# Token tile 3 normalised from the transposed copy of x, query weights loaded later, one exponential behind a copy, one warm-up product fewer

## The chip, the cores and the metric

The kernel runs on one core of one Trainium2 chip. The metric is device time in microseconds (us) of one execution; the median of three runs stands for a kernel. The engines are TensorE (PE in the profile, its weight loads PEld), VectorE (DVE), ScalarE (ACT), GpSimd (POOL) and SyncE (SP), which here only issues transfers.

## The reference

x has 2048 tokens of 640 numbers. A linear attention with 32 heads of 20 and a gated MLP read the same layer norm of x:

```python
x = A_x
xn = _layernorm(x, axis=-1)
s = _A_ref(xn, A_wqkv, A_w_phi, A_wo)
g = _silu(_B_ref(xn, B_w1, B_b1, B_w2, B_b2))
return x + s * g
```

with, in `_A_ref`, after `q, k, v` have been made from `xn @ wqkv` and `pq`, `pk` from `q` and `k` by the head's matrix `w_phi`:

```python
phi_k = jnp.concatenate([_softmax(pk, axis=-1), _softmax(-pk, axis=-1)], axis=-1)   # phi_q alike
kv = jnp.einsum("bhsf,bhsd->bhfd", phi_k, v)
z  = jnp.einsum("bhsf->bhf", phi_k)
num = jnp.einsum("bhqf,bhfd->bhqd", phi_q, kv)
den = jnp.einsum("bhqf,bhf->bhq", phi_q, z)[..., None] + 1e-6
o = num / den
```

`_B_ref` is `gelu(xn @ w1 + b1) @ w2 + b2` with 1536 hidden numbers. All inputs are float32.

## The kernel before

Tokens are worked in 16 tiles of 128, tile t being half of pair q = t // 2 (`at(q)` is the pair's place). Products are made in split form: each operand is a high part (rounded, `AF.Copy` on ScalarE into float32r) and a low part (the rest, a subtraction on VectorE or GpSimd), and `PASSES` adds high x high, high x low and low x high. In `project` a block of x is the weight side: for each of five blocks, four passes read its high part and then two its low part. The order of instructions is written out by hand on every engine in this part of the program (`tc.manual_schedule`), so each engine works in the order of the code.

The start of the program, up to about 240 us of the profile, is attention:

- Nine products of ones by ones (L521) run first on TensorE. The key weights are folded with `w_phi` on TensorE (`fold`, L174) from `wkT`, loaded by `load_fold(1, ...)`; the right side is a block matrix `foldb` that VectorE makes (L542) of the loaded `bd`.
- Tiles 0 to 3 are loaded as rows of tokens (`x_in`), normalised there (`norm_a`/`norm_b`/`norm_act`; L246 is the VectorE form), transposed on TensorE (`transpose_x`, L363) and split from PSUM (`plain`, L285 and L287). Tile 3 goes through `norm(3)` and is transposed within the value projection of tile 1.
- Tiles 4 and later come in pairs: `load_xr` brings x already transposed, `pair_stats` makes mean and reciprocal root (the power of -1/2 on GpSimd, L233) from the row copy, writes them to `st_dram` (L337) and reads them back broadcast to all partitions (`bc`, L339); `pair_sub` (GpSimd, L346) and `pair_mul` (VectorE, L351) normalise, `pair_plain` splits.
- A key tile: `project` (L377), `feat1` (VectorE: maximum L389, difference L392, minimum L395; GpSimd: the negated half L396), `feat2` (exponential on ScalarE, L405), `key_fin` (sums L413 and reciprocal L445 on VectorE, scaling L418 on GpSimd). A value tile: `project`, then a copy (L434). `kv_pair` multiplies the two (L457).
- The query weights, `wqT = load_fold(0, ...)`, are loaded near the head of SP's queue, after tiles 1 to 5 and the value weights; `fold_pair` first reads them after tile 4.
- Tiles 10 to 15 make their values by a shorter scheme in pairs (`token_pair`, L685), into whose seven parts other work is hung by `hooks`. Hook 1 is `rest`: the negated half of the later key, the exponential of the first, and more. The value copy of part 2 (L694) comes behind it on ScalarE.

After that stand the MLP (L924 first layer, L953 second layer) and the output projection (L1111), which the change doesn't touch.

```python
vs[1] = value(1, lambda: transpose_x(3))
phis[1] = key_fin(es.pop(1))
vf = [v_forms(0), v_forms(1)]
for t in range(2, 6):
    pk = project(t, wk_s)
```

Of the kernel before, what the change touches and what calls it, by code (L numbers as in the profile page):

```python
# [15 lines left out]
P = 128  # L16
# [13 lines left out]
NH = 2  # L30
# [16 lines left out]
def hedgehog_gated_mlp_kernel(ctx: ExitStack, tc: tile.TileContext, x, xt_in, wqk, bd, wv, wo, w1, b1, w2, b2, out_t):  # L47
# [39 lines left out]
    def bankA():  # L87
        return pools["A"].tile([P, 2, 512], F32, tag="A", name="pA")
# [72 lines left out]
    def load_fold(which, engs):  # L161
        tl = folds[:, which]
        for c, eng in enumerate(engs):
            if c == 1 and which:
                x_in(0, nc.scalar)
            eng.dma_start(tl[:, c], wqk[which, c, :, :6 * P].rearrange("p (i t) -> p i t", i=6))
        return tl
# [185 lines left out]
    def pair_plain(q):  # L353
        for o in range(2):
            plain(q, o, xrs[q][:, :, o * P:(o + 1) * P])

    def transpose_x(t):
        q, o = divmod(t, 2)
        xn = xns.pop(t)
        ps = bankA()  # L360
        flat = ps[:].rearrange("p a b -> p (a b)")
        for k in range(KC):
            nc.tensor.transpose(flat[:, k * P:(k + 1) * P], xn[:, k * P:(k + 1) * P], ident[:])  # L363
        plain(q, o, flat[:, :D].rearrange("p (k t) -> p k t", t=P))
# [148 lines left out]
    def x_in(t, eng=None):  # L513
        xts[t] = load_x(t, eng)
# [1 line left out]
    phase1 = ExitStack()  # L516
    phase1.enter_context(tc.manual_schedule(engines={mybir.EngineType.PE, mybir.EngineType.SP}))
    one = nc.const_aps.tensor(1.0, [P, P], F32)
    for pw in (bankA(), bankA(), bankA()):
        for i in range(3):  # L520
            nc.tensor.matmul(pw[:, 0, :P], one, one, start=True, stop=True)  # L521
    startup = ExitStack()
    startup.enter_context(tc.manual_schedule())
# [4 lines left out]
    wv_raw = [load_raw(wv[c * P:(c + 1) * P, :]) for c in range(KC)]  # L528
    for t in (3, 4, 5):
        x_in(t)  # L530
    wqT = load_fold(0, (nc.sync,) * KC)
    x_in(6)
    x_in(7)
    nc.sync.dma_start(b1t[:], b1)
# [25 lines left out]
    es[0] = feat1(pk)  # L560
    split_v(3)
    pk = project(1, wk_s, lambda: transpose_x(2))
    load_xr(2)
    load_xr(3)
    x_in(8)
    x_in(9)
    load_xr(4)
    split_v(4)
    feat2(es[0])
    norm(3)  # L570
    es[1] = feat1(pk)
    pair_stats(4)
    vs[0] = value(0)
    pair_stats(5)
    phis[0] = key_fin(es.pop(0))
    feat2(es[1])
    vs[1] = value(1, lambda: transpose_x(3))
    phis[1] = key_fin(es.pop(1))
    vf = [v_forms(0), v_forms(1)]
    for t in range(2, 6):  # L580
        pk = project(t, wk_s)
        if t % 2:
            kv_pair(t - 3)
        es[t] = feat1(pk)
        if t == 4:
            next(vf[0])
        if t == 2:
            pair_sub(2)
            pair_stats(6)
            pair_stats(7)  # L590
            pair_mul(2)
        if t == 3:
            pair_plain(2)
        if t > 3:
            pair_stats(t + 4)
        if t in (3, 4, 5):
            spill(t - 3)
        if t == 5:
            x_in(10)
        if t == 4:  # L600
            pair_sub(3)
            pair_mul(3)
        vs[t] = value(t, (lambda: transpose_x(t + 2)) if t < 2 else None)
        if t >= 4:
            fold_pair(t - 4)
        if t == 5:
            next(vf[0])
        feat2(es[t])
        if t == 4:
            pair_plain(3)  # L610
        phis[t] = key_fin(es.pop(t))
# [182 lines left out]
    for p in range(5, 8):  # L794
# [21 lines left out]
        def rest(t=t, p=p):  # L816
            if p == 5:
                nc.scalar.dma_start(e_dram[_tok(queries_done.pop(0))], ef)
                next(vb)
                next(vb, None)  # L820
            later.pop(0)()
            feat2(es[t])
            if p == 6:
                t_sums(7)
            if p == 7:
                next(qf)

# [10 lines left out]
            if p == 6:  # L838
                t_split(7)

        value_pair(p, {1: rest, 2: lambda: p == 7 and next(qf), 3: lambda: p == 5 and pair_sub(7), 4: first_key, 6: second_key})
    w1f = w1_forms(w1r)

    def early_rest(q, ea):
# [522 lines left out]
```

## Time and profile before

| | |
|---|---|
| median of three runs | 651.21 us (651.04 to 651.24) |
| the profiled execution | 651.21 us |
| its span, first to last instruction | 649.3 us |
| granted TensorE clock, mean | 0.999 |
| busy: PE, DVE, ACT, POOL | 644.2, 483.1, 237.9, 406.8 us |
| DMA | 136.07 MB, mean 210 GB/s |

A row of the timeline reads: start in us, length in us, engine, line, operation, what is written `<-` what is read, shapes, how many were merged, and in brackets how long the engine was idle before and what ended that. A row of the chain reads: start, length, engine, tile, line, count. In a row of waits stand the waiting engine, tile and line, `<-` the one waited for, total us, times, and the longest. A row of a table by stretches has the stretch, its length, busy time and count of PE, PEld, DVE, ACT and POOL, the granted clock, the DMA share and GB/s. SPq and ACTq are the issuing sides of those engines, on which a row is the issue alone.

### The profile page before, as it was taken

Reading aid. Unit: us, or ns where it says so; the run is one execution under the profiler, and the core shown is the slowest. Engines: PE = TensorE matmul, PEld = TensorE weight load, DVE = VectorE, ACT = ScalarE, POOL = GpSimd, SP = SyncE. Lnnn points to the kernel's source line nnn. Section 1 sums busy time; section 2 is a strip of 40 time slices with the busy share of each in tenths; the row PEclk is TensorE's granted clock in tenths of the full one; section 3 lists DMA queues with packets and bytes.
Section 4 is the critical chain, followed back from the end, with each engine's and each line's share of the span. In section 5 each row is a group of like instructions: output and inputs, shape, how many; then the busy total and the mean of one; then the engine's idle time right before and its main releaser. Section 6 shows DMA issues by size and latency. Waiting matters only on the chain.

```text
span 649.3 us, 11414 instructions
## 1 busy us (share of the span) xinstructions
PE 644.2 (99%) x4384; PEld 559.6 (86%) x4384; DVE 483.1 (74%) x736; ACT 237.9 (37%) x345; POOL 406.8 (63%) x373
## 2 busy tenths in 40 slices
PE   9999999999999999999999999999999999999997
PEld 9999999999999998888888888888888886766866
DVE  5886976789777887587988877768889899853232
ACT  3522423325243447144243356642231524032130
POOL 2776477897986756857878875455462966343321
PEclk9999999999999999999999999999999999999999
DMA  8918186494312477365987999694969499999952
GB/s 346 327 18 220 43 299 200 114 300 148 123 42 66 160 263 254 111 213 172 311 234 246 253 411 280 136 344 181 184 228 251 63 279 207 319 244 244 275 192 81
DMA packets 166175, 136.07 MB, mean 210 GB/s; under 512 B 89714, under 2 KB 130162, under 8 KB 165738
## 3 DMA queue, kind: packets, MB, share of 16 engines
q1 hardware_dynamic: 163386, 123.76, 65.7%
q10 hardware_dynamic: 2736, 11.60, 4.7%
q8 instruction: 34, 0.56, 0.4%
q14 instruction: 19, 0.16, 0.1%
HBM read 86.95 MB, written 48.38 MB: 208 GB/s over the span
## 4 chain that ended last, share of the span: by engine, by line
PE 97%; DVE 2%; ACT 0%; issue 0%; POOL 0%; DVEq 0%; POOLq 0%
PE pB L953 24%; PE pA L377 23%; PE pB L924 23%; PE pB L1111 11%; PE pA L685 6%; PE pA L174 2%; PE pB L1058 2%; PE kv L457 2%; PE qV L685 1%; PE qY L685 1%; PE pA L521 1%; DVE y L962 1%; PE pB L1065 1%; PE pA L363 0%; DVE wolh L1035 0%; DVE den L1012 0%
## 5 line engine op out<-in xcount | busy, mean ns | idle before, releaser
L953 PE MATMUL pB<-hs,w2s 128*128 128x512 f32 x720 | 165.8, 389 | 0.0
L953 PEld LDWEIGHTS pB<-hs,w2s 128*128 128x128 f32 x720 | 135.0, 188 | 28.8 <-DVE y L962 0.8
L924 PE MATMUL pB<-xp,w1s 128*128 128x512 f32 x324 | 81.2, 389 | 0.0
L924 PE MATMUL pB<-xd,w1s 128*128 128x512 f32 x324 | 79.3, 389 | 0.0
L1111 PE MATMUL pB<-oT,wo 128*128 128x512 f32 (+1 forms) x315 | 72.3, 381 | 0.0
L418 POOL TENSOR_TENSOR eq<-eq,rc 128x1280 f32<-128x1280 f32 x16 | 37.9, 2370 | 54.6 <-DVE rc L1015 36.7
L924 PEld LDWEIGHTS pB<-xd,w1s 128*128 128x128 f32 x324 | 60.8, 188 | 12.6
L924 PEld LDWEIGHTS pB<-xp,w1s 128*128 128x128 f32 x324 | 60.8, 188 | 12.6
L1111 PEld LDWEIGHTS pB<-oT,wo 128*128 128x128 f32 x315 | 57.2, 188 | 13.8 <-PE pB L1058 2.5
L962 DVE TENSOR_TENSOR y<-pB,y 128x512 f32<-128x512 f32 x100 | 63.1, 675 | 1.4 <-PE pB L953 1.4
L929 ACT ACTIVATE pB<-pB,b1t 128x512 f32<-128x512 f32 x48 | 31.8, 662 | 78.7 <-DVE pB L1192 28.9
L405 ACT ACTIVATE e<-e 128x1280 f32<-128x1280 f32 x32 | 40.8, 1273 | 52.2 <-POOL e L396 52.2
L377 PE MATMUL pA<-wk,xp 128*128 128x320 f32 x384 | 59.6, 310 | 0.0
L396 POOL TENSOR_TENSOR e<-nr,e 128x640 f32<-128x640 f32 x32 | 45.6, 1425 | 20.3 <-DVE nr L395 20.2
L377 PEld LDWEIGHTS pA<-wk,xp 128*128 128x128 f32 x384 | 56.9, 188 | 0.1
L418 POOL TENSOR_TENSOR e<-e,rc 128x1280 f32<-128x1280 f32 x16 | 37.9, 2372 | 19.1 <-DVE rc L445 19.1
L1002 POOL TENSOR_TENSOR ez<-eq,zrep 128x1280 f32<-128x1280 f32 x16 | 47.3, 2957 | 2.7 <-DMA eq<-e_dram 2.7
L485 POOL TENSOR_TENSOR w1s<-raw,w1s 128x640 fp32r<-128x640 f32 (+1 forms) x18 | 26.3, 1460 | 27.0 <-ACT w1s L484 27.0
L377 PE MATMUL pA<-wv,xp 128*128 128x320 f32 x240 | 37.2, 310 | 0.0
L1114 POOL TENSOR_TENSOR xres<-gt,xres 128x256 f32<-128x256 f32 x20 | 14.3, 736 | 35.3 <-DVE gt L1113 35.3
L149 POOL TENSOR_TENSOR w2s<-raw,w2s 128x640 fp32r<-128x640 f32 x23 | 36.0, 1587 | 0.2 <-ACT w2s L147 0.2
L377 PEld LDWEIGHTS pA<-wv,xp 128*128 128x128 f32 x240 | 35.5, 188 | 0.1
(182 smaller groups left out, 1137.2 us busy)
## 6 DMA issues: line engine op xcount, KB each, us to landing
raw<-in_w_dram SPq DMA_DIRECT2D x42, 320.0 KB
e_dram<-e ACTq DMA_DIRECT2D x16, 640.0 KB
eq<-e_dram SPq DMA_DIRECT2D x16, 640.0 KB
phi_t<-eq SPq DMA_DIRECT2D x64, 160.0 KB
phT<-phi_t SPq DMA_DIRECT2D x20, 480.0 KB
xt<-in_x_dram SPq DMA_DIRECT2D x16, 320.0 KB
xres<-in_xt_dram SPq DMA_DIRECT2D x20, 256.0 KB
out_dram<-xres SPq DMA_DIRECT2D x18, 256.0 KB
```

The source lines that it names most:

```text
L149: eng.tensor_tensor(sl[:, 1, :], raw, sl[:, 0, :].bitcast(F32), op=OP.subtract)
L377: nc.tensor.matmul(ps[:, hf, :HALF], stat_x(q, o, k, a), ws[k][:, b, hf * HALF:(hf + 1) * HALF], start=n == 0, stop=n == 3 * KC - 1)
L396: rest = lambda: nc.gpsimd.tensor_tensor(e5[:, :, :, 1, :], nr[:, :, :, None].to_broadcast([P, 2, 16, DH]), e5[:, :, :, 0, :], op=OP.subtract)
L405: nc.scalar.activation(ef, ef, AF.Exp)
L418: nc.gpsimd.tensor_tensor(e3, e3, rc[:, :, None].to_broadcast([P, 64, DH]), op=OP.mult)
L685: nc.tensor.matmul(bank[ch], q_x(blk, a, q), p_weight(base, f, w, k)[:, b], start=ch not in seen and n == 0, stop=n == len(mms) - 1, skip_ ...
L924: nc.tensor.matmul(bank[ch][:], tl[:, a, off + wo_:off + wo_ + P], mov(blk, b), start=new and n == 0, stop=n == len(mms) - 1, skip_group_c ...
L929: nc.scalar.activation(ps, ps, AF.Gelu_apprx_tanh, bias=b1t[:, f:f + 1])
L953: nc.tensor.matmul(ps[:], ws[i][:, b, d * P:(d + 1) * P], hs[o][i][:, a, :], start=i == n == 0, stop=(i, n) == (GF - 1, 2), skip_group_che ...
L962: nc.vector.tensor_tensor(y, ps[:], y, op=OP.add)
L1002: nc.gpsimd.tensor_tensor(zv, ef, zf, op=OP.mult)
L1111: nc.tensor.matmul(ps[:, mv], w, o[:, mv], start=n == 0, stop=n == 15, skip_group_check=True)
```

## The change

1. Tile 3 is no longer normalised as rows and transposed. Its half of the transposed x is loaded (`one_load`), its statistics go through DRAM and come back broadcast (`one_stats`), GpSimd subtracts (`one_sub`), VectorE multiplies and the split is made from SBUF (`one_plain`). The five transposes are gone.
2. The query weights, the rows of tiles 8 and 9 and the transposed x of pairs 3 and 4 are asked for behind the statistics of tile 3 and of pair 2.
3. In the value pairs the first key's exponential moves from hook 1 to hook 2, behind the copy of part 2. For pair 7 a step of the query forms moves with it.
4. Eight products of ones instead of nine.

```diff
+    def one_load(t):
...
+        nc.sync.dma_start(xr[:, :, :P], src)
+        xrs[t, "one"] = xr[:, :, :P]
+
+    def one_stats(t):
+        sm = small.tile([P, 16], F32, tag="st", name="st")
+        ps = small.tile([P, 2], F32, tag="ps1", name="ps1")
+        stats(t, sm, ps[:, 0:1], ps[:, 1:2])
+        nc.sync.dma_start(st_dram[t // 2, t % 2], ps[:])
+        bc = row([P, P, 2], F32, "bc")
+        nc.sync.dma_start(bc[:].rearrange("p t s -> p (t s)"),
+                          st_dram[t // 2, t % 2].rearrange("p s -> (p s)").partition_broadcast(P))
+        pld[t, "one"] = bc
+
+    def one_sub(t):
+        bc, xr = pld[t, "one"], xrs[t, "one"]
+        nc.gpsimd.tensor_tensor(xr, xr, bc[:, None, :, 0].to_broadcast([P, KC, P]), op=OP.subtract)
+
+    def one_plain(t):
+        bc, xr = pld.pop((t, "one")), xrs.pop((t, "one"))
+        nc.vector.tensor_tensor(xr, xr, bc[:, None, :, 1].to_broadcast([P, KC, P]), op=OP.mult)
+        plain(t // 2, t % 2, xr)
...
-    for pw in (bankA(), bankA(), bankA()):
-        for i in range(3):
+    for pw, n in ((bankA(), 3), (bankA(), 3), (bankA(), 2)):
+        for i in range(n):
...
-    wqT = load_fold(0, (nc.sync,) * KC)
...
+    one_load(3)
     load_xr(2)
-    load_xr(3)
-    x_in(8)
-    x_in(9)
-    load_xr(4)
     split_v(4)
     feat2(es[0])
-    norm(3)
+    one_stats(3)
     es[1] = feat1(pk)
     pair_stats(4)
     vs[0] = value(0)
     pair_stats(5)
+    one_sub(3)
+    wqT = load_fold(0, (nc.sync,) * KC)
+    x_in(8)
+    x_in(9)
+    load_xr(3)
+    load_xr(4)
     phis[0] = key_fin(es.pop(0))
     feat2(es[1])
-    vs[1] = value(1, lambda: transpose_x(3))
+    vs[1] = value(1)
     phis[1] = key_fin(es.pop(1))
+    one_plain(3)
...
             later.pop(0)()
-            feat2(es[t])
             if p == 6:
                 t_sums(7)
+            if p == 7:
+                next(qf)
+
+        def copied(t=t, p=p):
+            feat2(es[t])
             if p == 7:
                 next(qf)
...
-        value_pair(p, {1: rest, 2: lambda: p == 7 and next(qf), 3: lambda: p == 5 and pair_sub(7), 4: first_key, 6: second_key})
+        value_pair(p, {1: rest, 2: copied, 3: lambda: p == 5 and pair_sub(7), 4: first_key, 6: second_key})
```

On VectorE, between the sums of keys 0 and 1 (`rc`) and the maximum of key 2 (`mx`), there stands before (`b_298` is the part of the pair's high and low halves kept beside `xp`, `pA` a PSUM bank):

```order
L413 TENSOR_REDUCE rc<-e 128x64
L445 RECIPROCAL rc<-rc 128x64
L287 TENSOR_TENSOR b_298<-pA,b_298 128x2x128
L287 TENSOR_TENSOR xp<-pA,xp 128x3x128
L413 TENSOR_REDUCE rc<-e 128x64
L445 RECIPROCAL rc<-rc 128x64
L389 TENSOR_REDUCE mx<-pA 128x32
```

and after the change, at the same place:

```order
L440 TENSOR_REDUCE rc<-e 128x64
L472 RECIPROCAL rc<-rc 128x64
L440 TENSOR_REDUCE rc<-e 128x64
L472 RECIPROCAL rc<-rc 128x64
L381 TENSOR_TENSOR xr<-xr,bc 128x5x128
L287 TENSOR_TENSOR b_292<-xr,b_292 128x2x128
L287 TENSOR_TENSOR xp<-xr,xp 128x3x128
L416 TENSOR_REDUCE mx<-pA 128x32
```

The two low parts of tile 3 read `xr` in SBUF where they read `pA` in PSUM, a multiplication precedes them, and all three stand behind both keys' sums.

On GpSimd, from the power of -1/2 for tiles 4 and 5 (`pst`) to the scaling of key 1, there stands before:

```order
L233 TENSOR_TENSOR pst<-pst,mhalf 128x1
L427 MEMSET v 128x32
L428 MEMSET v 128x32
L233 TENSOR_TENSOR pst<-pst,mhalf 128x1
L418 TENSOR_TENSOR e<-e,rc 128x1280
```

and now:

```order
L233 TENSOR_TENSOR pst<-pst,mhalf 128x1
L454 MEMSET v 128x32
L455 MEMSET v 128x32
L233 TENSOR_TENSOR pst<-pst,mhalf 128x1
L377 TENSOR_TENSOR xr<-xr,bc 128x5x128
L445 TENSOR_TENSOR e<-e,rc 128x1280
```

The subtraction of tile 3 stands ahead of the scaling of key 0, and so of all that follows.

On SP, from the last loads of x rows at the start, there stands before (`folds` are the query weights, `xr` the transposed x, `st_dram` and `bc` the statistics' way out and back):

```order
L142 DMA xt<-in_x_dram 128x640 x3
L166 DMA folds<-in_wqk_dram 128x768 x5
L142 DMA xt<-in_x_dram 128x640 x2
L534 DMA b1t<-in_b_dram 128x12
L535 DMA b2t<-in_b_dram 128x5
L266 DMA xr<-in_xt_dram 128x5x128
```

and now:

```order
L142 DMA xt<-in_x_dram 128x640 x5
L560 DMA b1t<-in_b_dram 128x12
L561 DMA b2t<-in_b_dram 128x5
L362 DMA xr<-in_xt_dram 128x5x128
L266 DMA xr<-in_xt_dram 128x5x128
L267 DMA xr<-in_xt_dram 128x5x128
L369 DMA st_dram<-ps_370 128x2
L371 DMA bc<-st_dram 128x256
L337 DMA st_dram<-pst 128x2x2
L339 DMA bc<-st_dram 128x512
L166 DMA folds<-in_wqk_dram 128x768 x5
```

The query weights come behind two write-and-read pairs of statistics, the first of them tile 3's.

6 lines of the change are left out of this document (5 added, 1 removed).

## The prediction

> **What bounds the kernel now.** The page first, its engines and its chain of work that ended last; then the waits of TensorE; then that chain between 16 and 64 us.
>
> ```profile
> PE 644.2 (99%) x4384; PEld 559.6 (86%) x4384; DVE 483.1 (74%) x736; ACT 237.9 (37%) x345; POOL 406.8 (63%) x373
> ```
>
> ```profile
> PE 97%; DVE 2%; ACT 0%; issue 0%; POOL 0%; DVEq 0%; POOLq 0%
> ```
>
> ```profile
> PE pA L521 <- PEq L1357: 0.8, 1, 0.8
> PE pB L1065 <- DVE y L962: 0.4, 1, 0.4
> PE pA L685 <- ACT v L694: 0.2, 1, 0.2
> ```
>
> ```profile
> 21.35 8.80 PE pA L377 x60
> 30.15 0.55 PE pA L363 x5
> 30.70 14.96 PE pA L377 x102
> ...
> 60.35 2.67 PE pA L174 x24
> ```
>
> TensorE waits 1.4 us in all. So time is won only by taking work from it, at most what is taken, and lost wherever an operand now comes later than TensorE does. 60 passes of L377 in 8.80 us are 0.147 us each. The profiled execution took 651.21 us for a span of 649.3 us; that is also the median of the three runs, so what the sum changes in the span is added to 651.21.
>
> **Transposes.** Five L363 passes of tile 3 go from the chain: 0.55 us by the row above, and nothing takes their place on TensorE.
>
> **Warm-up product.** The nine products are 18 passes in 4.18 us, so one is worth up to 0.46.
>
> ```profile
> 0.84 4.18 PE L521 MATMUL pA<-const-float32-1.0 128*128 128x128 f32 x18 [0.84 <-PEq L1357]
> 4.08 0.98 DVE L542 TENSOR_TENSOR folds<-folds 120x120 f32<-120x120 f32 x2 [4.08 <-DMA folds<-in_bd_dram]
> 5.11 0.91 PEld L174 LDWEIGHTS pA<-folds 120*128 120x128 f32 x4
> ```
>
> The second L542 operation makes the block matrix of the second fold product; it ends at 5.06 and that product's weights load at 5.11. Its start hangs on a transfer, not on TensorE, so products that end sooner only wait for it. I take 0, between -0.46 and +0.46 (a slower start of the clock by as much).
>
> **The exponential.** In the value pair of tiles 10 and 11:
>
> ```profile
> 164.89 1.27 ACT L405 ACTIVATE e<-e 128x1280 f32<-128x1280 f32 x1 [0.75 <-POOL e L396]
> 165.32 1.04 PE L685 MATMUL pA<-wv,xd 128*128 128x320 f32 x6
> 166.07 0.42 ACT L694 ACTIVATE v<-pA 128x320 f32<-128x320 f32 x1
> 166.54 0.71 PE L685 MATMUL pA<-wv,xd 128*128 128x320 f32 x3 [0.18 <-ACT v L694]
> ```
>
> Six passes from 165.32 end their turn at 166.20; the next starts at 166.54, behind a copy that stood behind the exponential. With the copy in front, 0.34 us goes. The exponential itself starts only when GpSimd is done (164.89), so behind the copy it is hardly later; the two other pairs have no such wait, and are costed at 0 (the key's sums that follow have the rest of the pair to hide in).
>
> **Query weights.** Five loads of 384 KB move from the start of SP's queue to behind two statistics round trips. At the rate of the start
>
> ```profile
> 5.00:11.00 6.00, 6.00 (x51) 6.00 (x50) 4.08 (x9) 2.13 (x4) 0.56 (x1) 1.00 1.03 411
> ```
>
> 2 MB take some 5 us. SP now waits for tile 3's write, then for that of pair 2 (about 30.4), and with these for its own reads (29.2 and 33.6); the loads queue behind all that. Issued from about 34 us, they land by 43; the first fold that reads them is the chain's row at 60.35. Cost 0; without those 17 us, TensorE would wait for what is missing. Pair 2's broadcast, behind tile 3's, is asked for at 33.6 and not read before 44. The loads of x tiles 8 and 9 and of pairs 3 and 4 follow them, 3 us more, still ahead of 60.
>
> **Tile 3.** Its split (high part, low part) used to come from PSUM behind the transposes. Now the statistics go to DRAM and back, GpSimd subtracts, VectorE multiplies, ScalarE and VectorE split out of SBUF. First the arrival.
>
> ```profile
> 26.12 0.61 DVE L246 TENSOR_SCALAR xt<-xt,st 128x640 f32<-128x640 f32 x1 [1.25 <-POOL st L233]
> ```
>
> ```profile
> 25.55 0.54 POOL L233 TENSOR_TENSOR st<-st,mhalf 128x1 f32<-128x1 f32 x1
> 33.87 2.37 POOL L418 TENSOR_TENSOR e<-e,rc 128x1280 f32<-128x1280 f32 x1 [1.55 <-DVE rc L445]
> 39.51 1.28 POOL L396 TENSOR_TENSOR e<-nr,e 128x640 f32<-128x640 f32 x1 [0.54 <-DVE nr L395]
> ```
>
> ```profile
> 32.34 0.37 SPq L337 DMA_DIRECT2D st_dram<-pst  x1
> 35.47 0.34 SPq L339 DMA_DIRECT2D bc<-st_dram  x1
> 45.86 0.36 SPq L337 DMA_DIRECT2D st_dram<-pst  x1
> 49.20 0.33 SPq L339 DMA_DIRECT2D bc<-st_dram  x1
> ```
>
> ```profile
> 33.50:36.90 3.40, 3.40 (x25) 3.40 (x25) 2.92 (x6) 0.00 (x0) 2.80 (x4) 1.00 0.05 2
> 36.90:39.25 2.35, 2.35 (x18) 2.35 (x17) 2.28 (x3) 0.00 (x0) 2.07 (x1) 1.00 0.72 112
> ```
>
> The reciprocal root is still made on GpSimd at 25.55 to 26.09, and SP writes it at 26.1. The write is done when the read behind it is issued: 3.13 and 3.34 us in the two pairs. Half the bytes change little of that; I take 3.13. A broadcast of 256 KB begins to move 1.43 us after its issue and moves for 2.35 (112 GB/s). For 128 KB I take 1.43 + 1.5 and 0.5 until it is seen: 3.4, between 2.9 (bytes halved, seen soon) and 4.1 (as large as now). So it lands at 32.65. VectorE meanwhile is some 1.9 us ahead (the wait of 1.25 and L246's 0.61 are gone), so both keys' sums are done by 33.7.
>
> Now the order: GpSimd's subtraction stands ahead of both key scalings (L418), VectorE's three operations ahead of the maximum of key 2 (L389). And these three, unlike those that they replace, take two operands from SBUF. What that costs beside GpSimd:
>
> ```profile
> 20.66 1.56 POOL L149 TENSOR_TENSOR wv<-raw,wv 128x640 fp32r<-128x640 f32 x1 [0.29 <-ACT wv L147]
> 22.18 1.86 POOL L396 TENSOR_TENSOR e<-nr,e 128x640 f32<-128x640 f32 x1
> ```
>
> ```profile
> 21.36 1.55 DVE L149 TENSOR_TENSOR wv<-raw,wv 128x640 fp32r<-128x640 f32 x1
> ...
> 68.33 0.81 DVE L287 TENSOR_TENSOR xp<-xr,xp 128x640 fp32r<-128x640 f32 x1
> 69.06 0.42 DVE L287 TENSOR_TENSOR b<-xr,b 128x256 fp32r<-128x256 f32 x1
> ```
>
> Alone, 128x640 takes 0.81 (68.33). At 21.36, begun while a GpSimd operation ran to 22.22, it took 1.55: it ended 0.69 after that one. GpSimd's next took 1.86 where L396 alone takes 1.28 (39.51): it waited in turn. So one waits out the other, in the order of asking. [...]
>
> Step by step, with 1.57 for the subtraction (L346 does the same shape):
>
> ```profile
> L346 POOL TENSOR_TENSOR xr<-xr,bc x8: 1562/1592/1614, 40.7 to 123.1; 128x640 f32<-128x640 f32 x8
> L351 DVE TENSOR_TENSOR xr<-xr,bc x4: 1482/1492/2550, 43.9 to 124.7; 128x1280 f32<-128x1280 f32 x4
> ```
>
> Subtraction 32.7 to 34.27; scaling of key 0 right behind it, 34.25 to 36.62. The multiplication, due at 34.3, finds GpSimd busy: it ends 0.69 after 36.62, at 37.3. ScalarE's high parts follow by 37.75. Scaling of key 1 holds the port 37.3 to 39.55, so the first low part ends 0.3 after it, 39.85, the second 0.5 later, 40.3. Tile 3 itself is in time: 72 of the 102 passes from 30.70 stand ahead of its key projection, so that starts at 41.3 in before, 0.55 sooner now, and reads low parts from its fifth pass on. What is late is key 2:
>
> ```profile
> 36.89 0.82 DVE L389 TENSOR_REDUCE mx<-pA 128x32 f32<-128x640 f32 x1 [0.44 <-PE pA L377]
> ...
> 49.71 0.88 DVE L287 TENSOR_TENSOR xp<-xr,xp 128x640 fp32r<-128x640 f32 x1
> ```
>
> ```profile
> 51.39 1.78 PE L377 MATMUL pA<-wk,xp 128*128 128x320 f32 x11
> ```
>
> Its maximum starts at 40.25, 3.35 later. From there to the low parts of tile 4 (ended 50.59) VectorE and GpSimd hand work to each other almost without a gap: exponent half (39.51), subtraction and multiplication of pair 2, key sums, next key, split. So these end at 53.95. TensorE comes to tile 4 at 51.39 - 0.55 = 50.84, does four passes with the high part (0.59) and needs the low part at 51.43; with 0.05 for the signal it waits to 54.0. A new wait of 2.55.
>
> Sum: -0.55 - 0.34 + 0 + 0 + 2.55 = +1.66, so 652.9 us. With the round trip at its ends (2.9 + 3.1, and 4.1 + 3.34) it is +1.1 and +2.5. 0.2% is 1.3 us, about what a measurement of this kernel can tell from no change.
>
> **The rivals.** (1) No new wait: the multiplication gets the port before the scalings, or the round trip is quick. It decides where key 2's maximum starts no later than 37.7 (0.8 late: 51.43 against 50.64), that is with the broadcast landed by 30.1, or with no blocking. Then -0.89: 650.3. For it: 1.9 us won on VectorE. Against: 26.1 plus one write alone is 29.2, and the blocking stands in the rows. 0.19. (2) The same, and the warm-up product counts after all: -1.35, 649.9, just faster. Against it stands the row at 5.11. 0.08. (3) Worse: the broadcast lands at 33.6 and pair 2's multiplication is blocked as well (L351 reaches 2.55 where 1.49 is usual): +1.06 on +2.5 gives +3.5, 654.7, from the point where GpSimd starts another operation before that multiplication. [...] 0.12. (4) The change does not do what it says for tile 3, the wait being small (about 0.9) and eating the gain: 651.2, 0.05. The forecast keeps 0.56.
>
> **How the numbers follow.** Forecast 652.9, its own range 652.3 to 653.7 by the round trip. 650.3 to 654.2 takes in rival 1 and leaves out rivals 2 and most of 3, under 2 in 10. Slower by over 0.2% is above 652.5: three quarters of the forecast (0.43) and rival 3, 0.55; within: the rest of the forecast, rivals 1 and 4, 0.37; faster: rival 2, 0.08.
>
> **What would show it.** After: no L363 rows of tile 3; the first L174 weight load of the second product still near 5.11; SP's new write near 26.1 and its broadcast near 29.2; GpSimd's subtraction near 32.7; the multiplication about 3 us long, the 128x256 low part about 2; key 2's maximum near 40.2; TensorE waiting for VectorE's xp near 51.4 for 2.5 us; no wait for the value copy near 166. I am wrong if TensorE shows no new wait before 60 us, or if it sits at tile 3 instead.

## The result, and the profile after

The changed kernel takes 659.13 us (657.23 to 660.3, six runs) against 651.25 us of the kernel before, measured beside it (651.04 to 651.67, six runs): 1.0118 times as long, with a 95% interval of 1.0100 to 1.0136. The forecast was 652.9 us and a range of 650.3 to 654.2. It came slower, as forecast, but 6.2 us above the forecast and outside the range.

The profiled execution took 657.71 us, with a span of 655.9 us. Two lines of its page, the engines and the granted clock in 40 slices (tenths):

```profile
PE 647.3 (99%) x4377; PEld 559.7 (85%) x4377; DVE 488.5 (74%) x737; ACT 238.5 (36%) x345; POOL 409.0 (62%) x374
...
PEclk9998999999999999999999999999999999999999
```

TensorE has fewer passes than before (4377 against 4384) and is busy 3.1 us longer. One slice of the clock shows an 8 where before had none. The waits of TensorE in the changed kernel:

```profile
PE pA L404 <- DVE xp L287: 2.9, 1, 2.9
PE pA L548 <- PEq L1391: 0.8, 1, 0.8
PE pA L174 <- DMA folds<-in_wqk_dram: 0.4, 1, 0.4
PE pB L1099 <- DVE y L996: 0.3, 1, 0.3
PE pA L174 <- DVE folds L568: 0.2, 1, 0.2
```

The wait for the value copy (0.2 before) is gone, and a wait of 2.9 us for tile 4's low parts has come. (The 0.4 us for `folds` stand at 8.04 us, within the fold of the key weights; the query weights, which are now loaded later, are not waited for.) To see where the rest went, read the chain of waits of both kernels at the same pieces of work. Before, the first query fold starts at 60.35 (shown above), the projections of tiles 14 and 15 and the MLP at:

```profile
187.69 8.80 PE pA L377 x60
...
239.12 5.92 PE pB L924 x26
```

In the changed kernel the same chain has:

```profile
54.51 10.02 PE pA L404 x56
64.53 2.67 PE pA L174 x24
...
191.44 8.79 PE pA L404 x60
...
242.85 2.31 PE pB L958 x10
```

So it is 4.18 us behind at the fold, 3.75 at tiles 14 and 15, 3.73 where the MLP begins, and 6.6 at the end of the span. Two losses were not in the forecast: 4.18 is more than the wait, and 2.9 us come where the change edits nothing. Of these, 2.1 are lost in the MLP (5.82 behind at the first matmul of the output projection), 0.5 in the output projection (6.33 behind at its last matmul) and 0.3 after it.

**The first loss.** Stretches of the changed kernel, cut where its clock changes; the columns are stretch, length, busy time and count of PE, PEld, DVE, ACT and POOL, granted clock, DMA share and GB/s:

```profile
48.63:52.04 3.41, 2.98 (x21) 2.72 (x19) 3.34 (x5) 2.16 (x4) 1.83 (x4) 1.00 0.36 91
52.04:55.46 3.42, 0.95 (x6) 0.96 (x7) 3.39 (x4) 0.00 (x0) 3.42 (x2) 1.00 0.21 32
55.46:58.87 3.41, 3.41 (x15) 3.41 (x14) 2.79 (x4) 1.27 (x1) 0.25 (x3) 0.50 1.10 314
58.87:62.28 3.41, 3.41 (x25) 3.41 (x24) 2.17 (x4) 0.00 (x0) 2.37 (x1) 1.00 1.10 374
```

In the stretch after the wait the clock is at 0.50, and TensorE does 15 passes where the next stretch has 25. Half of 3.41 us is 1.7 us. With the wait and the transposes (-0.55 + 2.9 + 1.7 = 4.05) that makes the 4.18 nearly whole.

**The second loss.** Matmuls between 240 and 590 us, the mean ns of one in the last figure before the second bar; first of the kernel before, then of the changed one:

```profile
L953 PE MATMUL pB<-hs,w2s 128*128 128x512 f32 x720 | 165.8, 389 | 0.0
L924 PE MATMUL pB<-xp,w1s 128*128 128x512 f32 x321 | 80.5, 389 | 0.0
L924 PE MATMUL pB<-xd,w1s 128*128 128x512 f32 x324 | 79.3, 389 | 0.0
```

```profile
L987 PE MATMUL pB<-hs,w2s 128*128 128x512 f32 x720 | 166.3, 390 | 0.0
L958 PE MATMUL pB<-xp,w1s 128*128 128x512 f32 x324 | 82.2, 392 | 0.0
L958 PE MATMUL pB<-xd,w1s 128*128 128x512 f32 x324 | 80.0, 391 | 0.0
```

No wait appears here and the clock is 1.00; each matmul that streams xp or xd is 2 to 3 ns longer, in all twelve units of the MLP (a unit is one round through both layers; the second layer's matmuls, which stream `hs`, are about 0.7 ns longer too, and why they are is open). In the compiled program xp begins at byte 157952 of a partition before and at 158016 after: the new statistics tile `ps1` has two buffers of 32 bytes in the pool that lies ahead of xp, and xd and the buffers that later take their place move by the same 64 bytes. Both kernels also hold a pad tile of 64 bytes ahead of xp, and a second one ahead of those later buffers.

**The last 0.3 us.** From the end of the last VectorE operation to the end of the span it is 2.73 us before and 3.02 after. SyncE's wait for the last store, before and then after:

```profile
SPq L1363 <- DMA out_dram<-xres: 1.2, 1, 1.2
```

```profile
SPq L1397 <- DMA out_dram<-xres: 1.5, 1, 1.5
```

SyncE closes the program with six waits for transfers, in the same order in both traces and some 0.06 us each. Before, the last store is the last of the six, and the other five are over when it lands (so the wait for it starts 0.3 later). After, with three more transfers in SyncE's queue, the last store signals the semaphore that stands first in the list, and the other five follow its landing. The 3.0 us are there in all eight kernels run here that take tile 3's new path, and the 2.7 in all ten others; no run changes this order alone.

### The profile page after: what moved, and what is told of

Its sections match the earlier page's. It is cut to its first block, busy times and chain, and to the rows that moved or that the text cites. A ratio compares the mean times of both kernels' runs of the same rounds, so it can differ in the third digit from the quotient of the medians.

```text
span 655.9 us, 11407 instructions
## 1 busy us (share of the span) xinstructions
PE 647.3 (99%) x4377; PEld 559.7 (85%) x4377; DVE 488.5 (74%) x737; ACT 238.5 (36%) x345; POOL 409.0 (62%) x374
## 4 chain that ended last, share of the span: by engine, by line
PE 90%; DVE 5%; issue 2%; POOL 2%; DMA 1%; ACT 0%; SPq 0%; DVEq 0%; POOLq 0%; ACTq 0%
PE pB L987 23%; PE pB L958 22%; PE pA L404 18%; PE pB L1145 11%; PE pA L715 6%; PE pB L1092 2%; PE pA L174 2%; PE kv L484 1%; PE qV L715 1%; DMA folds<-in_wqk_dram 1%; PE qY L715 1%; POOL e L445 1%; DVE y L996 1%; PE pB L1099 1%; POOL xr L346 0%
## 5 line engine op out<-in xcount | busy, mean ns | idle before, releaser
L404 PE MATMUL pA<-wk,xp 128*128 128x320 f32 x384 | 61.4, 315 | 2.9 <-DVE xp L287 2.9
L404 PEld LDWEIGHTS pA<-wk,xp 128*128 128x128 f32 x384 | 58.5, 192 | 3.2 <-DVE xp L287 3.2
```

The source lines that it names most:

```text
L404: nc.tensor.matmul(ps[:, hf, :HALF], stat_x(q, o, k, a), ws[k][:, b, hf * HALF:(hf + 1) * HALF], start=n == 0, stop=n == 3 * KC - 1)
```

## The experiments

Three theories were open. **Address**: the second loss comes from the 64 bytes. **Queue**: the wait at tile 4 comes from key 2's maximum standing behind tile 3's operations, which GpSimd holds up. **Clock**: the first loss is the clock after that wait. Against them stood that the added slab moved all later slabs (slabs are large buffers of one pool, handed out in turn as a ring; rows are a ring of smaller ones), that the path is simply too long, and that the later load of the query weights costs. All runs have the kernel before beside them; "before" is its median there.

**Address 1.** The changed kernel without the pad tile ahead of xp.

```diff
-    xpool.tile([P, 16], F32, name="xpad")
```

> The changed kernel without its 64-byte pad tile ahead of xp: the new statistics tile (two buffers, 64 bytes of a partition) pushed xp and xd 64 bytes along, off a multiple of 128, and this puts them back. Theory (address): the FFN stage's matmuls return to 389 ns from 391 to 392, a unit of the stage to 25.84 us from 26.03, and the whole to about 659.1 - 2.8 = 656.3 us; the wait ahead of tile 4's key projection stays at 2.9 us. Rival (the slab ring stands one place further because of the added load, or the chip of the day): nothing changes, 659.1 us and 391 to 392 ns.

Measured: 655.13 us (653.51 to 655.49, five runs; before 651.07), 1.0052 with 1.0038 to 1.0066. The rows of the first layer (W1) are back at 389 ns, and the 2.9 us wait stays:

```profile
L957 PE MATMUL pB<-xp,w1s 128*128 128x512 f32 x324 | 81.3, 389 | 0.0
```

The address theory holds for the MLP, and the ring is out there. The five runs fall into two groups: 653.51 and 653.88 with a mean clock of 1.0 and 0.999, and 655.13 to 655.49 with 0.997. One stretch at half clock lowers the mean by 0.26%, so by their mean clocks the groups are runs without and with it.

**Address 2.** The kernel before with only the pad larger.

```diff
-    xpool.tile([P, 16], F32, name="xpad")
+    xpool.tile([P, 32], F32, name="xpad")
```

> The kernel before, with nothing but the pad tile ahead of xp twice as large, so that xp and xd lie where the change put them; same instructions, no added load. Theory (address): +2.8 us, 654.0 us, all of it behind 239 us, W1 rows at 391 to 392 ns. Rival (slab ring or chip): 651.2 us, 389 ns.

Measured: 653.41 us (653.08 to 653.72), before 651.07, 1.0035 (1.0023 to 1.0048), with W1 rows at 392 (xp) and 391 ns (xd):

```profile
L924 PE MATMUL pB<-xp,w1s 128*128 128x512 f32 x322 | 81.7, 392 | 0.0
```

One number in one pad, with no instruction changed, costs 2.34 us by the medians; in its trace 2.1 us are lost in the MLP, as in the changed kernel, and none behind it.

**Exponential alone.** The kernel before with `feat2(es[t])` behind the copy and nothing else.

```diff
-            feat2(es[t])
...
+        def copied(t=t, p=p):
+            feat2(es[t])
...
-        value_pair(p, {1: rest, 2: lambda: p == 7 and next(qf), ...
+        value_pair(p, {1: rest, 2: copied, ...
```

> The kernel before, with only the late pairs' first exponential moved behind the copy. Theory: the wait of 0.34 us ahead of the value pair's fifth product goes and nothing follows it: 650.9 us. Rival (a late exponential holds up the key sums behind it and a wait of its size comes back later): 651.2 us.

Measured: 650.96 us (650.63 to 651.5), before 651.07, 0.9997 (0.9988 to 1.0006). Not resolved. Its trace says why: TensorE was 0.50 us ahead of before at 169 us and 0.17 at 187. The timeline in between, VectorE and then GpSimd; first two rows of before, then three of this run:

```profile
176.34 1.65 DVE L351 TENSOR_TENSOR xr<-xr,bc 128x1280 f32<-128x1280 f32 x1
```

```profile
176.60 2.53 POOL L396 TENSOR_TENSOR e<-nr,e 128x640 f32<-128x640 f32 x1
```

```profile
175.84 3.30 DVE L351 TENSOR_TENSOR xr<-xr,bc 128x1280 f32<-128x1280 f32 x1
```

```profile
171.84 4.71 POOL L418 TENSOR_TENSOR e<-e,rc 128x1280 f32<-128x1280 f32 x2
176.49 1.30 POOL L396 TENSOR_TENSOR e<-nr,e 128x640 f32<-128x640 f32 x1
```

Pair 7's multiplication was asked for 0.5 us earlier. In both kernels it is asked for while the key scaling runs, before GpSimd's next operation. Before, it got in as the scaling ended and GpSimd's next operation waited (2.53 instead of 1.30). Now GpSimd went straight on to its next operation at 176.49, and the multiplication, which stood from 175.84, ended at 179.14, 1.35 after that one. What differs is that GpSimd's next operand (the minimum on VectorE) was ready 0.62 us before the scaling ended, and 0.23 before the change; whether that decides is not shown. The split and the first value copy behind it came too late for TensorE by 0.3. The gain was real and most of it was given back 12 us later by which of the two operations went first; the rival of that run was right about where it goes.

**Earlier chain.** Tile 3's chain begun 6 us earlier, and its multiplication ahead of the key sums, at the old address of xp.

```diff
     norm_a(2)
+    one_load(3)
+    one_stats(3)
...
-    one_load(3)
...
-    one_stats(3)
+    one_sub(3)
     es[1] = feat1(pk)
...
     pair_stats(5)
-    one_sub(3)
+    one_plain(3)
...
-    one_plain(3)
```

> The changed kernel at the old address of xp, with tile 3's chain earlier: its statistics right behind tile 2's (VectorE was idle from 16.62 to 18.00 us), the subtraction ahead of the second key's span on GpSimd, the multiplication and the low parts ahead of the key sums instead of behind them. Theory (the wait at tile 4 comes from key 2's maximum standing in VectorE's queue behind a multiplication and low parts that GpSimd's key scaling holds up): the multiplication takes about 0.75 us instead of 2.97, key 2's maximum starts near 37 us instead of 40.77, no wait ahead of tile 4's projection, granted clock 1.00 all through, and the time is 651.2 - 0.53 (transposes) - 0.34 (exponential) = 650.4 us. Rival (the transposed path itself is too long for this place, wherever it starts): a wait of over 1 us stays before 60 us and the time is over 652 us.

Measured: 651.32 us (650.92 to 651.83), before 651.07, 1.0003 (0.9994 to 1.0012). No wait between 1 and 160 us, no stretch at half clock there. VectorE in this run:

```profile
29.73 1.88 DVE L380 TENSOR_TENSOR xr<-xr,bc 128x640 f32<-128x640 f32 x1 [1.58 <-POOL xr L376]
32.09 0.42 DVE L286 TENSOR_TENSOR b<-xr,b 128x256 fp32r<-128x256 f32 x1 [0.48 <-ACT b L284]
...
36.89 0.76 DVE L415 TENSOR_REDUCE mx<-pA 128x32 f32<-128x640 f32 x1
```

The same three in the changed kernel, and GpSimd beside them:

```profile
34.89 2.97 DVE L381 TENSOR_TENSOR xr<-xr,bc 128x640 f32<-128x640 f32 x1 [1.02 <-POOL xr L377]
38.35 2.03 DVE L287 TENSOR_TENSOR b<-xr,b 128x256 fp32r<-128x256 f32 x1 [0.48 <-ACT b L285]
...
40.77 0.81 DVE L416 TENSOR_REDUCE mx<-pA 128x32 f32<-128x640 f32 x1
```

```profile
33.23 1.63 POOL L377 TENSOR_TENSOR xr<-xr,bc 128x640 f32<-128x640 f32 x1 [2.70 <-DMA bc<-st_dram]
34.82 2.37 POOL L445 TENSOR_TENSOR e<-e,rc 128x1280 f32<-128x1280 f32 x1
...
37.26 2.83 POOL L445 TENSOR_TENSOR e<-e,rc 128x1280 f32<-128x1280 f32 x1
```

In the changed kernel the multiplication ends 0.67 us after the first scaling and the low part 0.29 after the second: each ended only when GpSimd was done. With no scaling beside it the low part takes 0.42. (The multiplication takes 1.88 here and not 0.75: it ends at 31.61, 0.69 after GpSimd's negated half of key 1, but has the time.) Key 2's maximum is back at 36.89, where it was before the change. So the wait comes from when and where tile 3's operations stand; the next run tells the two apart. The time missed (650.4 expected): the trace was 1.11 us ahead at 169 us and 0.75 through the MLP, having lost 0.35 at pair 7 as above; then 0.47 went in the output projection and 0.3 in the closing waits.

**Key 2 first.** The changed kernel at the old address of xp with one call moved.

```diff
-    one_plain(3)
     vf = [v_forms(0), v_forms(1)]
     for t in range(2, 6):
         pk = project(t, wk_s)
...
         if t == 2:
+            one_plain(3)
             pair_sub(2)
```

> The changed kernel at the old address of xp, with one edit in VectorE's order: key 2's maximum, subtraction and minimum ahead of tile 3's multiplication and low parts instead of behind them. Theory (the order in VectorE's queue makes the wait): key 2's maximum starts near 36.3 us, the wait of 2.9 us at tile 4 is gone, and a shorter one of 0.5 to 1.5 us stands at tile 3's key projection near 40.4 us, too short for the clock to fall: granted clock 1.00, 651.0 to 652.0 us. Rival (the added work itself is too much for VectorE before tile 4, in either order): a wait near 51 us stays, with 653 us or more.

Measured: 652.92 us (651.97 to 653.54), before 651.28, 1.0025 (1.0015 to 1.0034); clock 0.999 and above in all eight runs. Key 2's maximum starts at 36.25. The big wait is gone; 0.3 us stand at tile 3 and 0.5 at tile 4 (from start to start). The order in VectorE's queue makes the wait. That is the queue theory's picture in size and place, with a time 0.9 above its range: the trace was 0.22 behind before at 169 us, 0.58 behind pair 7, 1.15 at the last matmul and 1.46 at the end of the span, lost at pair 7, in the output projection and in the closing waits again.

**Tile 3 undone.** The changed kernel with `norm(3)` and `transpose_x(3)` put back and no `ps1`; exponential, eight products and the later load stay.

```diff
-    one_load(3)
...
-    one_stats(3)
+    norm(3)
...
-    one_sub(3)
...
-    vs[1] = value(1)
+    vs[1] = value(1, lambda: transpose_x(3))
...
-    one_plain(3)
```

> The changed kernel with tile 3 put back on normalization and transposes; eight warm-up products, the later load of the query weights and the moved exponential stay, and the pad tile keeps xp at its old address. Theory (all of the loss hangs on tile 3's path and its statistics tile): no wait over 0.4 us before 160 us, granted clock 1.00, the time that of the exponential alone, 650.7 to 651.1 us. Rival (the later load, queued on SP ahead of tiles 8 and 9, costs something that tile 3's wait covers): over 651.5 us, with a wait at the first query fold near 60 us.

Measured: 650.83 us (650.36 to 652.32), before 651.28, 0.9995 (0.9986 to 1.0004). No wait at the first query fold: the later load costs nothing, and all the loss hangs on tile 3's path and its tile. It has the lowest median of all kernels run; below before by less than can be told.

**Slab ring.** The early version with tile 3's copy of x in a row buffer.

```diff
-        xr = slab(F32, "xr", (P, KC, W2))[:]
+        xr = row([P, KC, P], F32, "xr1")[:]
...
-    one_load(3)
-    one_stats(3)
+    one_stats(3)
+    one_load(3)
```

The first two lines are against the changed kernel; the rest is against the early version, whose statistics now also come ahead of the load.

> The early version with tile 3's transposed copy in a buffer of the row ring instead of the slab ring, so that every later slab keeps its place of before. Theory (the added slab moved all later slabs one place, and in two of the four output chunks a matmul then took 232.6 ns from start to start instead of 228.3, 80 and 111 of them, 0.33 + 0.15 us): both chunks return to 228.3 ns and the time falls by 0.4 to 0.5 us, to 650.7 to 650.9 us. Rival (those chunks are slow by chance of the run, or for another reason): 232 ns and 651.3 us.

Measured: 651.46 us (650.87 to 652.98), before 651.28, 1.0008 (0.9998 to 1.0017), with the two chunks (the second and the fourth) still at 232.7 ns. The ring theory fell. The weights of the output projection, `wo`, lie in buffers of the pool that takes xp's place at the end, and so do the head outputs of the first and third chunk. The second pad of 64 bytes stands ahead of that pool; with only the first pad out, these buffers still began 64 bytes further on than before.

**Both pads.** The changed kernel without either pad.

```diff
-    xpool.tile([P, 16], F32, name="xpad")
...
-            ctx.enter_context(tc.tile_pool(name="pad", bufs=1)).tile([P, 16], F32, name="lpad")
```

> The changed kernel without either pad tile, so that xp, xd and the late buffers (among them the heads' output tiles of two of the four output chunks) all begin on a multiple of 128 bytes as before. Theory (the 232.7 ns of those two chunks, which stayed when tile 3's copy left the slab ring, come from the late buffers' 64 bytes, not from the ring): 228.4 ns in all four chunks, 0.5 us below the version with one pad, 654.6 us where the clock falls and 653.1 where it does not; what is left over the kernel before is tile 4's wait and the clock. Rival (the chunks depend on the ring or on the chip): 232.7 ns, 655.1 us.

Measured: all four chunks at about 228 ns. Page lines of the changed kernel and of this one:

```profile
L1145 PE MATMUL pB<-oT,wo 128*128 128x512 f32 (+1 forms) x315 | 72.8, 383 | 0.0
```

```profile
L1144 PE MATMUL pB<-oT,wo 128*128 128x512 f32 (+1 forms) x315 | 72.3, 381 | 0.0
```

The time is 654.87 us (653.41 to 657.16), before 651.3, 1.0055 (1.0037 to 1.0073). Three runs have 653.41 to 653.56 at a mean clock of 0.999, two have 656.19 and 656.22 at 0.997, one 657.16 at 0.994. So the undisturbed cost of the change without its addresses is 2.2 us.

Which operand was it? In the compiled program the slow chunks stream their head outputs from slabs, which did not move; what moved by 64 bytes under them is `wo`. In the first and third chunk streamed operand and weights both moved by 64 bytes, and their matmuls are no slower from start to start (227.6 and 228.2 ns, before 227.8 and 228.3; the two slow chunks have 232.5 and 232.6, before 228.3 and 228.2). By the chain the first and third chunk take 14.57 and 18.48 us, before 14.59 and 18.47. In the MLP it is the streamed operand that moved and the weights that stayed.

**Waits of chosen length.** The kernel before with n statistics operations on VectorE ahead of tile 4's low parts; n = 8, then 11 and 6.

```diff
         if t == 3:
+            sm = small.tile([P, 16], F32, tag="st", name="st")
+            for _ in range(n):
+                nc.vector.bn_stats(sm[:, :6], xts[8][:, :HALF])
             pair_plain(2)
```

> The kernel before with eight extra statistics operations on VectorE (0.4 us each from start to start) ahead of tile 4's low parts, so that TensorE waits about 8 * 0.4 - 1.25 = 1.95 us there; nothing else differs. Theory (the clock is set by how idle TensorE was in a window of about 3.4 us that runs free of the wait; the changed kernel's wait of 3.05 us was followed by 3.41 us at half clock in some runs only): with 1.95 us no window is idle enough, clock 0.999 to 1.0 in all runs, 651.1 + 1.95 = 653.0 us, all runs within 0.8 us. Rival (any wait of a couple of microseconds lets the clock fall): runs at 0.997 and 654.7 us among them.

Measured with eight: each took 0.53 us, so TensorE waited 2.5 us rather than 1.95. 654.10 us (653.91 to 655.55), before 651.28, 1.0052 (1.0039 to 1.0065): three runs at 653.91 to 654.10 with clock 0.999 to 1.0, two at 655.54 and 655.55 with 0.997. The theory fell in its number: the rival's two kinds of runs came (1.5 us apart), so a wait shorter than a window is enough.

> The kernel before with eleven extra statistics operations on VectorE ahead of tile 4's low parts (0.53 us each in the run with eight, where TensorE waited 2.7 us): TensorE waits about 2.7 + 3 * 0.53 = 4.3 us. Theory (windows of 3.41 us that run free of the wait; one in which TensorE stood still for about 2.3 us or more is followed by one at half clock, which costs 1.7 us): a wait of 4.3 us always leaves such a window, so every run is at 0.997 or below and near 651.3 + 4.4 + 1.6 = 657.3 us, with no run near 655.6. Rival (the fall is a chance of the run and not of the wait's length): two or three of five again.

Measured with eleven: a wait of 4.1 us; 657.73 us (657.21 to 658.74, four runs), before 651.3, 1.0099 (1.0086 to 1.0112), clock 0.994 to 0.997 in each: every run has the fall.

> The same with six extra operations, a wait of about 2.7 - 2 * 0.53 = 1.6 us. Theory (windows, about 2.3 us of standing still needed): no run below 0.999, all near 651.3 + 1.7 = 653.0 us. Rival (the fall is a chance of the run): some runs at 0.997 and 1.6 us higher.

Measured with six: a wait of 1.5 us; 653.18 us (652.98 to 653.94, seven runs), before 651.3, 1.0030 (1.0019 to 1.0040), clock 0.999 or 1.0 in each: no run has it.

Now the profiles cut into steps of 3.41 us, counted from where the clock changes in the same trace. Eleven operations (the clock falls at 54.23), eight, six, then the changed kernel without pads, in whose profiled run it did not fall:

```profile
50.82:54.23 3.41, 1.48 (x11) 1.21 (x9) 3.17 (x8) 1.86 (x2) 0.61 (x3) 1.00 0.96 246
54.23:57.64 3.41, 1.23 (x4) 1.23 (x5) 3.34 (x7) 0.00 (x0) 0.00 (x0) 0.50 1.09 310
57.64:61.06 3.42, 3.42 (x14) 3.42 (x14) 1.47 (x2) 0.00 (x0) 1.77 (x1) 0.50 1.09 348
```

```profile
50.70:54.11 3.41, 1.53 (x11) 1.27 (x9) 3.21 (x8) 1.86 (x2) 0.67 (x3) 1.00 0.95 252
54.11:57.52 3.41, 2.75 (x19) 2.76 (x20) 3.35 (x5) 0.00 (x0) 0.00 (x0) 1.00 1.10 318
```

```profile
50.76:54.17 3.41, 1.94 (x14) 1.67 (x13) 3.27 (x8) 1.86 (x2) 0.66 (x3) 1.00 1.03 261
```

```profile
49.18:52.59 3.41, 2.15 (x15) 1.89 (x13) 3.31 (x5) 1.89 (x4) 1.83 (x4) 1.00 0.07 7
52.59:56.01 3.42, 1.92 (x13) 1.92 (x14) 3.33 (x4) 0.81 (x1) 2.71 (x4) 1.00 0.76 129
```

A window with TensorE busy for 0.95 (the changed kernel) or 1.48 us is followed by half clock; one with 1.23 us keeps it there; one with 1.53, 1.92 or 1.94 us is not. The last kernel waited 2.8 us, but the border fell into the middle of the wait, and neither side was idle enough. The end of the program tells the same: TensorE runs out of work there, and a step with 1.37 us of it (the kernel before, from 644.25) is followed by half clock, one with 2.57 (the changed kernel, from 649.38) is not. So where the border falls into a wait would decide, and one kernel would have two kinds of runs; each kernel left only one profile, so both kinds were not seen of one.

**Best of both.** The early version without pads, and pair 7's split moved behind the first value copies.

```diff
-        if p == 6:
-            pair_plain(7)
...
             if p == 6:
+                pair_plain(7)
                 t_sums(7)
```

> The early version without either pad, and pair 7's high and low parts behind the first two copies of the value pair instead of ahead of them. Theory: transposes -0.55, exponential -0.45, nothing given back at pair 7 (where those parts, held up by a multiplication of 3.30 us, delayed the copies by 0.3) nor in the output chunks: 651.2 - 1.0 = 650.2 us, faster than the kernel before by 0.15%. Rival (the time of these kernels is set by more than TensorE's chain, or pair 7's parts are then late for the next projection): 650.8 us or more.

Measured: 651.60 us (651.27 to 652.2), before 651.3, 1.0006 (0.9997 to 1.0014). TensorE now waits 0.7 us for VectorE's `v` in that pair; the lead of 1.06 us at 169 is 0.06 at 187. The rival was right: the split is then in front of what VectorE adds for the values.

**Which addresses.** What was open here was whether 64 bytes cost because they are off a multiple of 128 or whether xp may not move at all: the kernel before with its pad 128 and 32 bytes larger (48 and 24 numbers instead of 16), and at last 256 (80 numbers).

```diff
-    xpool.tile([P, 16], F32, name="xpad")
+    xpool.tile([P, 48], F32, name="xpad")
```

> The kernel before with the pad ahead of xp 128 bytes larger, so that xp and xd are moved by 128 bytes and still begin on a multiple of 128. Theory (the remainder counts): W1 matmuls at 389 ns and 651.3 us as before. Rival (any move of xp against the other buffers costs): 391 to 392 ns and about 653.6 us.

> The kernel before with that pad 32 bytes larger. Theory (the remainder modulo 128 counts, whatever it is): as with 64 bytes, 391 to 392 ns and 653.6 us. Rival (only a remainder modulo 64 counts, and 64 was a chance): then 32 is off too, with the same time, and the run can't tell; if it is 651.3 us, 32 bytes are fine and only 64 hurts.

Measured: 655.45 us (655.17 to 655.65; 1.0065, 1.0052 to 1.0077) with 128 bytes and 655.83 (655.73 to 656.02; 1.0071, 1.0058 to 1.0085) with 32, before 651.23. A multiple of 128 is not the rule; that theory fell. Neither side had expected that 32 and 128 bytes cost more than 64.

> The kernel before with the pad ahead of xp 256 bytes larger. Theory (what TensorE streams must begin on a multiple of 256 bytes; 157952, where xp began, is one): 389 ns and 651.2 us. Rival (any move of xp against the other buffers costs): 391 ns or more and at least 653 us.

Measured: 651.21 us (651.04 to 651.57), before 651.21, 1.0000 (0.9991 to 1.0009). The W1 rows with xp at 32, 128 and 256 bytes:

```profile
L924 PE MATMUL pB<-xp,w1s 128*128 128x512 f32 x321 | 82.7, 395 | 0.0
```

```profile
L924 PE MATMUL pB<-xp,w1s 128*128 128x512 f32 x321 | 82.6, 395 | 0.0
```

```profile
L924 PE MATMUL pB<-xp,w1s 128*128 128x512 f32 x320 | 80.3, 389 | 0.0
```

157952 is 617 times 256. For xp a multiple of 256 is fast in both places tried; remainders 32, 64 and 128 cost 4.6, 2.3 and 4.2 us. That the streamed operand itself must begin on such a multiple does not follow, and the output projection speaks against it. The weights that are loaded beside xp lie in slabs, all on multiples of 256, so these runs move the distance between the two as well. A distance off a multiple of 256 fits the MLP and all four output chunks. It does not fit the attention stage, where xp is the weight side of matmuls of 320 numbers: they take 146.6 ns from start to start before the change and 146.7 after it, with xp 64 bytes further on. No run moved both operands in the MLP, so the rule stays open.

**Early version, clean.** The early version without pads, and nothing else.

> The early version without either pad, and nothing else. Theory (its trace was 0.76 us ahead at 187 us and lost 0.33 and 0.15 us in two output chunks, whose late buffers are now back in place): 228.4 ns in all chunks, clock 1.00 throughout, 0.75 us ahead to the end: 650.5 us. Rival (the added operations on VectorE and GpSimd cost elsewhere): 651 us or more.

Measured: 651.03 us (650.36 to 651.66), before 651.23, 0.9997 (0.9988 to 1.0006). Chunks at about 228 ns. It was 1.12 us ahead of before at 169 us and 0.10 at 187: pair 7's multiplication took 3.41 us there and TensorE waited 0.4 for a sum of the values. At the last matmul it is still 0.08 ahead, and after the closing waits 0.23 behind. Tile 3's path can be made harmless; a gain could not be measured.

## Why the prediction was wrong, step by step

**Transposes and the order of waits: right.** The wait came where it was put, at the tile 4 projection, for the reason given, and through the steps given. The multiplication was called 3 us long and the 128x256 low part 2; they are 2.97 and 2.03. Every sign in "What would show it" came, within 0.6 us. All of them lie before 170 us; of the 4.8 us that the profiled run took beyond the forecast, 2.9 come later. One reading was too simple: VectorE and GpSimd do not always go in the order of asking (pair 7, above). Tile 3's steps did not depend on it.

**Size of the wait: a little low.** 2.55 was said, 2.9 came. The mis-sized term is the time from the broadcast's issue to its use, taken as 3.4 with 4.1 as its end. SyncE in the changed kernel:

```profile
26.13 0.34 SPq L369 DMA_DIRECT2D st_dram<-ps  x1
28.99 0.34 SPq L371 DMA_DIRECT2D bc<-st_dram  x1
```

The write took 2.86 (3.13 said), but GpSimd's subtraction starts only at 33.23, 4.24 after the second issue; key 2's maximum stands at 40.77 rather than 40.25. No run shows the port of which the prediction speaks; what the runs showed is that the multiplication ended 0.67 us and the low part 0.29 after a scaling of GpSimd.

**Exponential, load, warm-up product: right in place.** The wait at the copy is gone. The exponential gained 0.45 rather than 0.34 (4.20 us behind ahead of that pair, 3.75 behind it). It stays a gain only where pair 7's multiplication does not lose its turn: the changed kernel kept it, alone it was given back in part. The later load cost nothing (tile 3 undone). The second fold product still waits for VectorE's block matrix, so the ninth product was worth nothing that shows: it starts at 4.91, and a later one then waits 0.42 for its key weights. TensorE does start slower: before, the passes of L174 take 0.155 us each up to 5.95 (6 in 0.93) and 0.100 behind it (17 in 1.70).

**The clock: the step that failed first.** The sum (-0.55 - 0.34 + 0 + 0 + 2.55) ends with the wait and prices it at its length; it has no term for the clock that TensorE has after it, and the forecast of a 2.5 us wait was not tested against that clock. The runs show steps of 3.41 us that are not tied to the program's start: counted back from where the clock falls, the first border lies 4.26 us after the first instruction in the changed kernel, 5.95 in the kernel before and 6.44 with eleven operations. TensorE need not stand still through a whole step: with 1.48 of 3.41 us busy the clock already fell. By the mean clocks, a wait of 2.5 us was followed by it in two of five runs, waits of 2.8 and 2.9 in three of six and three of five, and in five of six of the changed kernel; one of 4.1 in all four, one of 1.5 in none of seven. The missing term is 1.5 to 2.7 us, the distance between the two groups of runs in three kernels, times the share of runs that have it. Rival 3's own mechanism, pair 2's multiplication blocked, did not happen (it took 1.49).

**Addresses: the step that was not there.** The prediction put everything from the MLP on at nothing: it priced every instruction of `one_stats`, and neither its tile nor its transfers. Two buffers of 32 bytes cost 2.1 us in the MLP by the trace (2.3 by the medians, measured alone) and about 0.5 in the output projection (0.34 + 0.17 us in two chunks). Three more transfers cost 0.3 at the end.

Sum for the profiled run, against the kernel before: 3.73 up to the MLP (transposes, wait, half clock, exponential), 2.09 in the MLP, 0.51 in the output projection, 0.30 at the end are 6.63, all that its span is longer. For a run with no fall of the clock, 2.2 (the change without its addresses, closing waits included), 2.1 to 2.3 and 0.5 are 4.8 to 5.0, so 656.0 to 656.3 us; the fastest run, clock 0.999, took 657.23. 0.9 or more of it stays without a cause. With the clock at 0.995 to 0.997 the others took 657.71 to 660.3; why three lie at 0.995, as two windows would, is open, as only the run of 657.71 left a profile.

## What to carry to other kernels

Before an edit is costed, ask what its tiles move: a new tile in a shared pool shifts everything allocated behind it, and where that moves a matmul's streamed operand against its weights (by 32, 64 or 128 bytes here) a whole stage can slow down with no wait and no clock to show it, only a mean that is 2 to 6 ns longer. A TensorE wait is priced with the clock behind it: in these runs one of 1.5 us cost its length alone, one of 2.5 to 2.9 us cost 1.5 us or more on top in 13 of 22 runs; the median of such a kernel is a mixture, so look at single runs. A gain of a third of a microsecond on a bound engine can be lost later where an operation of VectorE ends behind one of GpSimd: 0.33 of 0.50 us went so at pair 7 here.

## What the runs showed of the hardware

- The clock changed in steps of 3.41 us: it stood at half for one (55.46 to 58.87 in the changed kernel) or for two (54.23 to 61.06 with eleven operations). The first border lay 4.26, 5.95 and 6.44 us after the program's first instruction (the changed kernel, before, eleven operations). It fell after steps with 0.95, 1.37 and 1.48 us of TensorE's busy time (the changed kernel, the end of before, eleven operations), and not after steps with 1.53, 1.92 and 1.94 us (eight operations, the changed kernel without pads, six operations).
- A matmul that streams 512 numbers in float32r from xp, with weights on a multiple of 256 bytes, took 389 ns by the profile with xp at a multiple of 256, 392 with a remainder of 64 and 395 with 32 or 128. In the output projection, with the weights at a remainder of 64, one took 232.5 ns from start to start with the stream at 0 (second chunk; before 228.3, both at 0), and 228.2 with the stream at 64 as well (third chunk; before 228.3). The attention stage, with matmuls of 320 numbers and xp as the weight side, took 146.6 ns before and 146.7 after, with xp at a remainder of 0 and of 64.
- A VectorE operation with both operands in SBUF, begun while a GpSimd operation ran, ended after it in the changed kernel: the multiplication of tile 3 (640 numbers, 2.97 us long) by 0.67 us and the 256-number low part (2.03 us, and 0.42 in the early version with no scaling beside it) by 0.29. At pair 7 the multiplication began before GpSimd's next operation in both kernels, and went first in one (before: 1.65 us) and second in the other (exponential alone: 3.30).
